# Projecting the queries of two token chunks as one Strassen pair, with three groups of loads held back until the keys have landed

## The chip, the cores and the metric

The kernel runs on one core of one Trainium2 chip. The metric is the device time of one execution in microseconds (us), lower being better. The span in a trace, from the first to the last instruction, is some 1.7 us shorter than that time.

## The reference

One transformer layer on 2048 tokens of width 1024, in bfloat16: layer norm, a projection to queries, keys and values, attention of 32 heads over 8 positions at a spacing of 2 (a token's own and seven earlier ones), an output projection with a residual, and a gated feed-forward part of inner width 3584 without an activation.

```python
qkv    = layernorm(x) @ wqkv                      # (2048 x 1024) @ (1024 x 3072)
idx    = pos[:, None] - 2 * arange(8)[None, :]    # 8 positions back from pos; negative ones masked
logits = einsum("bhsd,bhswd->bhsw", q, k[idx]) * 32 ** -0.5
o      = einsum("bhsw,bhswd->bhsd", softmax(logits), v[idx])
h      = x + o @ wo
# then, from layernorm(h): (g * u) @ w_down, with g = ln @ w_gate and u = ln @ w_up, added to h
```

## The kernel before

Tokens go in four chunks of 512. TensorE does all the matrix products. Attention itself runs on VectorE, a chunk at a time, out of a second layout: ScalarE evacuates q, k and v from PSUM, SyncE's queue stores them to device memory, and GpSimd's queue loads them back with heads and tokens spread over the 128 partitions. The result goes the same way: it is stored (`od`) and loaded transposed in quarters (`oT`), which the output projection reads. The order of everything is fixed when the kernel is built; work that isn't urgent sits in generators that are advanced as matmul groups are emitted. In the traces below each engine takes its instructions in that order (ScalarE's evacuations stood 8.30 us behind an issue, for instance), which the whole story turns on.

```python
# evacuation of one 128x512 group of q, k or v (ScalarE) and its store (SyncE)
def evac_qkv(c, m, ps):
    sg = t1k.tile([128, HB + TC], BF, ...)
    nc.scalar.copy(sg[:, HB:HB + TC], ps[:])
    ...
    nc.sync.dma_start(qd[c][...] or kd[c][...] or vd[c][...], ...)

# absolute sums over the down weights; the loads are issued by ScalarE itself
def abs_down():
    ring = wpool.tile([128, KO, 512], BF, tag="w", name="w_ring")
    def load(p):
        nc.scalar.dma_start(rows_of(p), wd_v[:, bass.ts(p, 4), 512:1024])
    for p in range(2):
        load(p)
    yield "later", 12.0
    for p in range(7):
        scale_d.add(p, rows_of(p), rows_of(p))          # ScalarE
        if p + 2 < 7:
            load(p + 2)
        yield "later", 4.9 * GROUP_US

# attention of one chunk, cut: products and sums to logits on VectorE, then
    nc.vector.tensor_tensor(lg[:], lg[:], mx..., ALU.subtract)
    nc.scalar.activation(lg[:], lg[:], ACTF.Exp, ...)   # the one step on ScalarE
    ...                                                 # sums, weights, products with v on VectorE
    nc.gpsimd.dma_start(od[c]..., oD[:])
    for cp in range(4):
        nc.gpsimd.dma_start(oT[:, :, cp, :], od[c][cp]...)

# the main order, cut
    qkv(0, range(1, 4))                 # block 0 came before; 0,1 are q, 2,3 k, 4,5 v
    load_qk(0)
    bg.finish(rows2)
    for t in range(4):
        norm1[2].transpose(t)           # SyncE
    xtiles[3] = load_x(3, "x", nc.sync)
    pump(6)                             # loads the value weights
    bg.add(norm1[3].sums(), bg.now + 18.0)              # chunk 3's layer norm, on ScalarE
    start_attention(0)
    sums = abs_down()
    bg.add(sums, bg.now + 25.0, first=True)
    qkv(1, range(4))
    qkv(0, range(4, 6))
    load_v(0)
    bg.add(norm1[3].rows(), bg.now, first=True)
    qkv(1, range(4, 6))
    ...
    qkv(2, range(6))
    qkv(3, range(4), last=True)         # each finished block frees a 1 MB slot for the next weights
    bg.finish(atts[0])
    nxt = wo_ln2(0)                     # first output projection and chunk 0's second norm
    qkv(3, range(4, 6), last=True)
```

## Time and profile before

| | before |
|---|---|
| time, median of 4 runs (span of those) | 770.38 us (770.09 to 770.49) |
| TensorE busy | 99% of the span |
| matmuls of q for chunks 2 and 3 | 128 of 512 columns |
| first output projection starts | 163.6 us |
| first quarter of its input lands | 147.97 us |
| second output projection starts | about 253.2 us |
| first quarter of its input lands | 248.09 us |

The prediction below shows the lines on what bounds this kernel. The timeline: start, length, engine and line, operation, output<-input, and in square brackets how long the engine had been idle and what released it. First ScalarE: the issue of two loads for the absolute sums, and the exponential of attention 0.

```profile
66.72 1.16 ACTq L671 DMA_DIRECT2D w_ring<-in_B_w_down_dram  x2
...
97.34 1.06 ACT L499 ACTIVATE lg<-lg 128x1024 f32<-128x1024 f32 x1
```

Then the first sum of the softmax on VectorE:

```profile
98.43 0.69 DVE L502 TENSOR_TENSOR trs<-lg 128x512 f32<-128x512 f32 x1 [1.12 <-ACT lg L499]
```

The issue of a load stands in ScalarE's own order like any other instruction. Here it cost ScalarE 1.6 us (the idle time of its next instruction, shown in the prediction), and VectorE waited 1.12 us for the exponential, hardly more than the 1.06 us that it lasts.

### The profile page before, as it was taken

What the parts mean: (1) busy time and instruction counts of PE and PEld (TensorE: products, weight loads), DVE (VectorE), ACT (ScalarE), POOL (GpSimd) and SP (SyncE); (2) the same over time, 40 slices, a digit from 0 to 9 for tenths busy, and PEclk for the clock granted to TensorE, in tenths of its full rate; (3) what the DMA queues carried; (4) which work ended last, traced back from release to release, by engine and by line L of the source; (5) the groups of instructions that cost most, each with busy time, mean ns of one, the idle gap of its engine ahead of it and who ended that gap; (6) DMA issues with size and microseconds to landing.
All of it is one profiled execution on the core that took longest, in us unless ns stands there. A gap on an engine that the chain in (4) does not pass through costs nothing.

```text
span 768.7 us, 10302 instructions
## 1 busy us (share of the span) xinstructions
PE 762.8 (99%) x3663; PEld 350.7 (46%) x3663; DVE 606.0 (79%) x718; ACT 513.1 (67%) x979; POOL 142.5 (19%) x152
## 2 busy tenths in 40 slices
PE   8999999999999999999999999999999999999998
PEld 5444444444444444444444444444444444444444
DVE  5639999999999999999998997975454444568863
ACT  4648966423687398778899986736777677788240
POOL 0000000200002000020000001018778677600000
PEclk9999999999999999999999999999999999999999
DMA  8999796999966699579559448674342423730001
GB/s 268 272 257 260 207 269 153 279 305 283 301 219 216 210 299 294 172 246 326 194 186 300 139 155 279 126 198 107 80 110 55 110 74 91 257 126 29 0 29 55
DMA packets 190915, 144.85 MB, mean 188 GB/s; under 512 B 81808, under 2 KB 181136, under 8 KB 188688
## 3 DMA queue, kind: packets, MB, share of 16 engines
q1 hardware_dynamic: 180416, 116.94, 54.2%
q0 software_dynamic: 3584, 22.02, 8.4%
q10 hardware_dynamic: 6864, 5.24, 2.5%
q8 instruction: 28, 0.46, 0.2%
q14 instruction: 23, 0.19, 0.1%
HBM read 110.10 MB, written 27.26 MB: 179 GB/s over the span
## 4 chain that ended last, share of the span: by engine, by line
PE 97%; DVE 2%; DMA 1%; issue 0%; ACTq 0%; DVEq 0%
PE ps L431 21%; PE dx L944 6%; PE pz L826 6%; PE pwu L431 6%; PE pu L431 6%; PE py L826 6%; PE pwg L431 6%; PE pg L431 6%; PE px L826 6%; PE wo L998 4%; PE pv L826 3%; PE ez L944 3%; PE ey L944 3%; PE ex L944 3%; PE dy L944 3%; PE wo L578 2%
## 5 line engine op out<-in xcount | busy, mean ns | idle before, releaser
L431 PE MATMUL ps<-lnT,w_qkv 128*128 128x512 bf16 x736 | 159.5, 379 | 0.0
L431 PEld LDWEIGHTS <-w_qkv 128*128 128x128 bf16 x736 | 71.9, 98 | 86.1 <-issue 0.2
L344 ACT CAST sg<-ps 128x512 bf16<-128x512 f32 x96 | 55.2, 586 | 46.9 <-PE ps L431 41.6
L477 DVE TENSOR_TENSOR prod<-qD,kD 128x4096 bf16<-128x4096 bf16 x32 | 72.2, 2284 | 12.8 <-DMA kD<-kd 12.8
L523 DVE TENSOR_TENSOR pv<-vD,at 128x4096 bf16<-128x4096 bf16 x32 | 72.4, 2285 | 0.2
L826 PEld LDWEIGHTS <-sw 128*128 128x128 f16 x448 | 43.8, 98 | 52.9 <-issue 0.2
L431 PEld LDWEIGHTS <-w_wu 128*128 128x128 bf16 x448 | 43.8, 98 | 52.9
L431 PEld LDWEIGHTS <-w_wg 128*128 128x128 bf16 x448 | 43.8, 98 | 52.9
L826 PE MATMUL px<-lnT,ws 128*128 128x512 bf16 x224 | 55.2, 379 | 0.0
L536 POOL DMA_DIRECT2D od<-oD x4 | 2.2, 544 | 275.6 <-DVE oD L534 275.6
L431 PE MATMUL pg<-lnT,w_wg 128*128 128x512 bf16 x224 | 52.9, 379 | 0.0
L431 PE MATMUL pu<-lnT,w_wu 128*128 128x512 bf16 x224 | 52.9, 379 | 0.0
L431 PE MATMUL pwu<-lnT,w_wu 128*128 128x512 bf16 x224 | 52.9, 379 | 0.0
L431 PE MATMUL pwg<-lnT,w_wg 128*128 128x512 bf16 x224 | 52.9, 379 | 0.0
L826 PEld LDWEIGHTS <-ws 128*128 128x128 f16 x336 | 32.9, 98 | 39.6
L807 POOL TENSOR_TENSOR sw<-ws 128x512 f16<-128x512 f16 x26 | 30.0, 1155 | 82.4 <-PE pv L826 49.1
L944 PEld LDWEIGHTS <-gs 128*128 128x128 f16 (+1 forms) x280 | 27.4, 98 | 33.0
L479 DVE TENSOR_TENSOR prod<-prod 128x4096 bf16<-128x4096 bf16 x16 | 36.6, 2288 | 0.4
L843 ACT COPY py<-px 128x512 f32<-128x512 f32 x28 | 16.0, 570 | 27.7 <-PE px L826 27.7
L808 POOL TENSOR_TENSOR sw<-sw,ws 128x512 f16<-128x512 f16 x26 | 30.0, 1154 | 2.0
L810 POOL TENSOR_TENSOR sw<-ws,sw 128x512 f16<-128x512 f16 x26 | 30.3, 1167 | 0.0
L809 POOL TENSOR_TENSOR sw<-ws 128x512 f16<-128x512 f16 x26 | 30.1, 1156 | 0.0
(334 smaller groups left out, 1472.9 us busy)
## 6 DMA issues: line engine op xcount, KB each, us to landing
w_wg<-in_B_w_gate_dram SPq DMA_DIRECT2D x14, 1024.0 KB, 6.9
w_wu<-in_B_w_up_dram SPq DMA_DIRECT2D x14, 1024.0 KB, 6.3
w_pair<-in_B_w_gate_dram SPq DMA_DIRECT2D x14, 512.0 KB, 4.0
w_pair<-in_B_w_up_dram SPq DMA_DIRECT2D x14, 512.0 KB, 5.3
w_wo<-in_A_wo_dram SPq DMA_DIRECT2D x6, 1024.0 KB, 7.6
w_qkv<-in_A_wqkv_dram SPq DMA_DIRECT2D x5, 1024.0 KB, 11.5
kd<-sg SPq DMA_DIRECT2D x32, 144.0 KB, 4.4
kD<-kd POOLq DMA_DIRECT2D x4, 1152.0 KB, 8.6
```

Of the source, the lines that this page charges most:

```text
L344: nc.scalar.copy(sg[:, HB:HB + TC], ps[:])
L431: nc.tensor.matmul(ps[:], lhsT=wt[:, ko, bass.ts(j, 128)], rhs=rhs[:, ko, :], start=(ko == 0), stop=(ko == KO - 1))
L477: nc.vector.tensor_tensor(prod[:, j], qD[:], kD[:, :, o:o + SUB], ALU.mult)
L479: nc.vector.tensor_tensor(prod[:, :, 0:16], prod[:, :, 0:16], prod[:, :, 16:32], ALU.add)
L523: nc.vector.tensor_tensor(pv[:, j], vD[:, :, o:o + SUB], at[:, w, None, :].to_broadcast((128, DH, SUB)), ALU.mult)
L807: eng.tensor_tensor(sw[:, i, 0], a21, a22, ALU.add)
L808: eng.tensor_tensor(sw[:, i, 1], sw[:, i, 0], a11, ALU.subtract)
L809: eng.tensor_tensor(sw[:, i, 2], a11, a21, ALU.subtract)
L810: eng.tensor_tensor(sw[:, i, 3], a12, sw[:, i, 1], ALU.subtract)
L826: nc.tensor.matmul(ps[:], lhsT=lhs[:, ko, :], rhs=rhs[:, ko, :], start=(fresh and ko == 0), stop=(ko == 3), skip_group_check=not fresh)
L944: nc.tensor.matmul(ps[:, bass.ds(lo, n)], lhsT=lhs[k][:, bass.ts(q, 128)], rhs=rhs[k][:, bass.ds(lo, n)], start=(fresh and k == 0), stop=( ...
L998: nc.tensor.matmul(ps[:], lhsT=oTs[c][:, kk, t, :], rhs=wts["wo", 2, hf][:, kk, :], start=(kk == 0), stop=(kk == KO - 1))
```

## The change

The intent is to save matmuls. Queries of chunks 2 and 3 are two products with the same weights, so they form a 2 x 2 block product, and Strassen's scheme needs 7 block products for 8. That takes sums of weights and of rows on VectorE, q weights scaled to float16 (so an absolute sum over them), and copies between PSUM banks. The pair needs the rows of both chunks and is placed behind the first output projection, which by the count of matmuls thereby comes 13.8 us earlier. The queries of chunk 2 come with it, so attention 2 is started behind it too. To get attention 0 started in spite of the added work, three groups of transfers that used to run beside the first k load now wait until it has landed. The core of the diff, cut at the dots:

```diff
-    qkv(0, range(1, 4))
-    load_qk(0)
+    qkv(0, [1], at={(1, k): (lambda k=k: q_abs(k)) for k in range(4)})   # 4 absolute sums, ScalarE
+    qkv(0, [2], at={(2, 2): scale_q.rows})
+    qkv(0, [3], at={(3, 2): scale_q.total, (3, 3): q_convert})
+    load_qk(0, after=lnTs[1][:, 0, TC - 1:TC])     # q load waits for chunk 1's transposes
+    start_attention(0)
+    qkv(1, [2])
     bg.finish(rows2)
+    w4 = wpool.tile([128, KO, 512], BF, tag="w", name="w_qkv_4")
+    nc.gpsimd.tensor_copy(w4[:, 0, 0:1], qkv_in["k", 0][:, 0, 0:1])      # the hold-back
+    pump(6, w4)
+    state["live"] += 1
+    xtiles[3] = load_x(3, "x", nc.sync)
     for t in range(4):
         norm1[2].transpose(t)
-    xtiles[3] = load_x(3, "x", nc.sync)
-    pump(6)
-    state["live"] += 1
-    bg.add(norm1[3].sums(), bg.now + 18.0)
-    start_attention(0)
+    bg.add(norm1[3].both(), bg.now + 20.0, first=True)   # sums and rows in one piece
     sums = abs_down()
-    bg.add(sums, bg.now + 25.0, first=True)
-    qkv(1, range(4))
+    bg.add(sums, bg.now + 18.0, first=True)
+    qkv(1, [3, 0, 1])
     qkv(0, range(4, 6))
     load_v(0)
-    bg.add(norm1[3].rows(), bg.now, first=True)
     qkv(1, range(4, 6))
 ...
-    qkv(2, range(6))
+    qkv(2, range(2, 6))
-    qkv(3, range(4), last=True)
+    qkv(3, range(2, 6), last=True)
     bg.finish(atts[0])
-    nxt = wo_ln2(0)
-    qkv(3, range(4, 6), last=True)
+    rows_q = q_row_sums()                          # 13 sums on VectorE
+    norm2 = [wo_norm(0, devs=False)]               # second norm of chunk 0, now on ScalarE
+ ...
+    for m0 in (0, 2):
+        q_pair(m0, room_q)                         # 2 x 2 Strassen blocks
```

## The prediction

> **What bounds the kernel now.** I read the page's busy shares first, then the chain that ended last, then everything the TensorE waited for, then single stretches of time.
>
> ```profile
> PE 762.8 (99%) x3663; PEld 350.7 (46%) x3663; DVE 606.0 (79%) x718; ACT 513.1 (67%) x979; POOL 142.5 (19%) x152
> ...
> PE 97%; DVE 2%; DMA 1%; issue 0%; ACTq 0%; DVEq 0%
> ```
> The TensorE is busy for 762.8 of 768.7 us, and 97% of the chain is its own work. That matmuls are merely in flight is not proof, so I looked at their spacing. In the chain in order of time (start, length, what):
>
> ```profile
> 27.20 136.41 PE ps L431 x632
> 163.61 13.81 PE wo L602 x64
> 177.42 13.81 PE ps L431 x64
> ```
> 136.41 us by 632 is 215.8 ns for each 128x512 matmul; 13.81 by 64 is the same. No pause separates the pieces, so from 27 to 191 us the array never waits. All its waits:
>
> ```profile
> PE warm_ps L338 <- DVE warm L324: 1.2, 1, 1.2
> PE pt L386 <- DVE ln L379: 0.8, 1, 0.8
> PE ps L392 <- DMA w_qkv<-in_A_wqkv_dram: 0.5, 1, 0.5
> PE ps L392 <- ACT lnT L387: 0.3, 1, 0.3
> ```
> All four fall in the first 16 us. So time is matmuls times spacing: a matmul removed gains 216 ns, and whatever makes the array wait costs its full length. There is nothing else to gain; the 12.8 us that VectorE idles at 39.6 to 52.3 cost nothing today.
>
> **What the skill says.** TensorE: Matmul & The Clock Gate, Back-to-back issue gap, gives N/2.4 + 2.5 ns for an isolated warm matmul, 215.8 for N=512; the trace agrees to the digit (its sustained 131 ns does not occur here). PSUM — Partial Sum Buffer, PSUM: the matmul accumulator, gives eight banks of 512 float32 columns; the kernel uses eight such tiles, so a product that can't get an evacuated bank waits. VectorE: DVE Perf Modes, The perf-mode tier table, gives a bf16 tensor_tensor of 2048 elements 1224 ns; the trace has 1222 (L481), so the Strassen sums are priced from it and from the 512-element float16 sums at 412 ns (L1112). DMA: Bandwidth & Descriptors, Issuing engines are not separate DMA queues, says that all transfers interleave on the same 16 engines. The trace agrees: chunk 1's first transpose landed 3.35 us after issue, the next, issued 0.4 us after the 1 MB q load, took 7.66.
>
> **The change: TensorE.** Before, q for chunks 2 and 3 is 2 chunks x 8 column tiles x 8 = 128 matmuls. After, it is 4 Strassen blocks x 7 products x 4 = 112. 16 fewer by 0.2158 = 3.45 us gained. One 64-column matmul for the weights' scale is added; at the 56 ns that 128 columns take in this trace, about 0.03. Net 3.42 us, that is 767.0 us if nothing waits.
>
> **ScalarE at the start.** Four absolute sums over the q weights are added, priced from this group, with the read of the accumulator 1.90 each, 7.6 in all:
>
> ```profile
> L635 ACT ACTIVATE w_ring<-w_ring 128x2048 bf16<-128x2048 bf16 x7 | 13.4, 1912 | 0.0
> ```
> They stand between the evacuations of 17 to 30 us, where ScalarE idled 3.6 us. It comes to issuing chunk 1's two late transposes at about 33.5 instead of 29.75 us. The recorded bank waits are all met: the tightest is the bank freed by the q evacuation at about 27.7, wanted at 30.5. The array wants chunk 1's transposes at 39.1. The old ones landed at 38.88, with 0.2 us to spare; the new second one goes at 34.9, and since the q load now waits for it, should take 3.4 and land at 38.3. No stall, 0.8 us of margin.
>
> **Start of attention.** The last k store goes 3 us later (43.1 for 40.04), its load issues at about 46.2 for 44.12. Freed of the 2 MB of value weights, 1 MB of rows and the transposes that come behind it now, it should take 6.8 for 8.12 and land at 53.0, where it landed at 52.24. VectorE has by then converted the q weights (2 x 1.25) and made 16 weight sums (6.1), ending at about 50.6, inside its old idle time. So the hold-back only pays for the delays.
>
> **The output projection is 13.8 us earlier.** 16 q groups (27.6) move behind it and 8 value groups (13.8) before it: it starts at 149.6, not 163.6. Attention 0 took 84.2 us of VectorE from the first product to the last sum (52.34 to 136.55), then 11.4 until the first transposed quarter landed (147.97). From 53.0: 148.6. Margin 1.0, where it was 15.6. The value weights should land near 63 for 66.7.
>
> **ScalarE in the Strassen pairs.** This is where I expect to lose. A bank is copied to the next by ScalarE inside each pair:
>
> ```profile
> L843 ACT COPY py<-px 128x512 f32<-128x512 f32 x28 | 16.0, 570 | 27.7 <-PE px L826 27.7
> L848 ACT ACTIVATE p<-pv,ibgu 128x512 f32<-128x512 f32 x28 | 19.2, 687 | 7.6 <-PE pv L826 7.6
> ```
> Two blocks take 56 matmuls, 12.1 us. On ScalarE they need 6 copies and 6 scaled evacuations, 12 x about 0.55 occupied = 6.6. In the same first 12 us the layer norm of chunk 0 now runs there instead of on VectorE: these pieces (chunk 3's norm, same shapes)
>
> ```profile
> 67.93 1.06 ACT L274 ACTIVATE njunk<-x 128x1024 bf16<-128x1024 bf16 x1 [1.60 <-DMA kd<-sg]
> 71.91 1.15 ACT L279 ACTIVATE njunk<-x,nroom 128x1024 bf16<-128x1024 bf16 x1
> 85.41 1.24 ACT L296 ACTIVATE ln<-x,nroom,rs 128x1024 bf16<-128x1024 bf16 x1
> ```
> give about 2.5 us a row tile for sum, mean and square, 1.3 for the four scales, 1.14 a row written. Three of the four row tiles are meant to be done in the projection. But each waits for VectorE's residual add, and VectorE runs late here:
>
> ```profile
> 167.89 4.49 DVE L477 TENSOR_TENSOR prod<-qD,kD 128x4096 bf16<-128x4096 bf16 x2
> 172.30 1.28 DVE L604 TENSOR_TENSOR h<-wo,h 128x512 bf16<-128x512 f32 x2
> ```
> The first add came 7.0 us after its group was done at 165.3. In the changed order it comes after 104.0 us of attention work, at 53.0 + 104.0 = 157.0, 5.7 late. The first row tile is then ready at 158.3, and three tiles end at 165.9. The first copy between banks is behind them, ends at 166.5, and is wanted at 166.0: 0.5 lost. The fourth tile (2.5) stands between two copies: the second block's third bank is ready at 171.8 for 170.9, 0.9 lost. The scales, then two written rows, cost about 0.1 each time. I laid the two queues end to end by hand: 1.7 us lost, pairs from 163.4 to 189.3 where 24.2 would do. VectorE's own row sums (12 x 0.4 + 1.2) end at 167.7, wanted at 168.3, so they just pass.
>
> **Sum.** 770.4 - 3.45 + 0.03 + 1.7 = 768.7; the rounded call is 768.6.
>
> **Rivals.** *Everything hides*: the order was made with care, and most margins above are positive by calculation; then 767.0. Against it: ScalarE has 6.6 + 2.5 + 1.3 + 2 x 1.14 = 12.7 us for 12.1 in the first pair, before any lateness. *ScalarE loses the whole gain*: if k lands 1 us later, at 54, every add is a microsecond later and the pairs lose about 3 us; with a microsecond from the transposes, 771. For it speak the 0.8 and 1.0 us margins, each worked out from one landing. *VectorE becomes the bound*: 15 us of conversions and sums plus 6 of evacuations are added, 8.4 of norm removed; the 12.8 us of idle take them up. It would enter the gated stage about 3.6 us later than before. The second projection has slack: its first quarter landed at 248.09 for 253.2. Minus the lateness and the 1.7 net shift, near zero remains; a miss would cost 0 to 2. *The hold-back itself gains*: k earlier frees VectorE, but VectorE idles off the chain, so no time.
>
> **Range and chances.** Floor 767.0 by the count of matmuls; executions differ by 0.14 us. The losses I add are 0 to 4 us, most likely 1 to 2.5. So 766.8 to 771.4 for 8 in 10. Two per cent is 15.4 us: the gain can't reach it, and a loss would need stalls of 19 us, a wait I missed altogether.
>
> **What would show it.** TensorE with 3648 matmuls. Its list of waits, empty after 16 us before, should show only the new bank tiles of the pairs (the y and z banks) released by ScalarE, 1 to 3 us in sum, and the pairs some 26 us long. The k load should land at 52 to 54 us. Chunk 1's matmuls and the first projection should start without a wait. It is wrong if the pairs take 24.2 us (copies in time), if the waits lie at the start (scale matmul, chunk 1's transposes, value weights) or at either projection, or if the sum of TensorE's waits is above 5 us.

## The result, and the profile after

The changed kernel takes 783.09 us (median of 4, 781.95 to 784.36); the kernel before took 770.38 in the same rounds. The ratio is 1.0166, with a 95% interval of 1.0148 to 1.0184. Ratios here are the mean time of one kernel's fast runs over that of the other's of the same rounds, so not quite the ratio of the medians. The class, within 2%, was as predicted; the sign was not, and 783.09 lies far outside 766.8 to 771.4.

The page of the changed kernel, busy shares and then the shares of the chain that ended last:

```profile
PE 763.7 (98%) x3648; PEld 349.7 (45%) x3648; DVE 620.9 (79%) x748; ACT 538.4 (69%) x1017; POOL 142.7 (18%) x154
...
PE 37%; DVE 35%; ACT 11%; DMA 6%; issue 5%; SPq 2%; ACTq 0%; DVEq 0%; POOL 0%; POOLq 0%
```

The count of 3648 matmuls is as predicted. But the chain now runs through TensorE for 37% only, where it was 97%. TensorE's busy time even rose by 0.9 us although it does 15 matmuls fewer: the page counts a matmul that runs slowly as busy too, which is 2.3 us here (below). The rest of the rise is not accounted for. TensorE's waits (engine, line and tile, what released it: total, times, longest):

```profile
PE wo L646 <- DMA oT<-od: 7.2, 1, 7.2
PE ps L480 <- ACT halo L399: 2.8, 2, 2.1
...
PE ez L1069 <- DVE hsr L787: 1.1, 1, 1.1
PE qz L934 <- ACT qz L974: 0.8, 1, 0.8
```

I also took the excess of each interval between starts of matmuls over 0.4217 ns a column. The large pieces are 2.25 us at 99.5 and 0.83 at 112.5 (a bank not evacuated by ScalarE), 7.36 at 153.1 (the first output projection, waiting for `oT`), 2.29 right behind it, 1.0 in the pair and 1.27 at 510. With a further 1.1 us of small pieces that is 16.1 us lost; 3.4 saved makes 12.7. The spans differ by 781.5 - 768.7 = 12.8.

The 2.29 us is a matter of clock: the granted clock was 0.86 of full speed from 160.6 to 177.0 us, where it was 1.00 in this stretch before. The projection's line in TensorE's timeline:

```profile
160.63 16.29 PE L646 MATMUL wo<-w_wo,oT 128*128 128x512 bf16 x64 [7.19 <-DMA oT<-od]
```

The same 64 matmuls took 13.81 us before. After the pause, ten of them started 426 or 427 ns apart instead of 216, and one 400.

Where `oT` came from, in the chain in order of time (start, length, what):

```profile
145.98 6.63 DMA od<-oD
...
153.17 7.41 DMA oT<-od
```

Attention 0 ended at 145.7 us, not at the predicted 137.2, and the trip through memory took 14.6 us from issue of the store to the first quarter. In the kernel before, GpSimd's timeline has the same issues closer together:

```profile
136.85 0.54 POOL L536 DMA_DIRECT2D od<-oD  x1 [47.11 <-DVE oD L534]
141.35 3.55 POOL L539 DMA_DIRECT2D oT<-od  x4 [3.96 <-DMA od<-oD]
```

There the store had landed at 141.06, and the first quarter at 147.97.

Attention 0 began about as predicted: the k load landed at 54.09 (predicted 53.0). The time went in the middle. VectorE:

```profile
97.90 1.23 DVE L551 TENSOR_TENSOR lg<-lg,mx 128x1024 f32<-128x1024 f32 x1
107.56 0.69 DVE L556 TENSOR_TENSOR trs<-lg 128x512 f32<-128x512 f32 x1 [8.44 <-ACT lg L553]
```

Its logits were ready at 99.1, and it then sat 8.44 us until the exponential was done. ScalarE, which owed it:

```profile
68.44 5.90 ACTq L674 DMA_DIRECT2D w_ring<-in_B_w_down_dram  x2
74.39 0.69 ACT L392 ACTIVATE sg<-ps,ibq 128x512 bf16<-128x512 f32 x1 [8.30 <-PE ps L480]
74.97 1.05 ACT L277 ACTIVATE njunk<-x 128x1024 bf16<-128x1024 bf16 x1
...
106.47 1.06 ACT L553 ACTIVATE lg<-lg 128x1024 f32<-128x1024 f32 x1
```

Read the second of these with care. ScalarE was idle for 8.30 us, and the line names TensorE as the releaser; but its group had been done for long. What stood there is the line above: the issue of the two w_ring loads, which the chain of waits shows released by a store of chunk 1's k. That store had stood in SyncE's queue, behind loads and transposes:

```profile
58.10 9.71 SPq L234 DMA_TRANSPOSE lnT<-ln  x4
67.92 2.65 SPq L406 DMA_DIRECT2D kd<-sg  x4
```

From 74.97 to the exponential ScalarE has no pause to speak of. It works through evacuations, absolute sums and the whole norm of chunk 3, four sums, four squares and four rows, all ahead of the exponential in its order. That order is not new: in the kernel before, too, the four rows (85.4 to 94.9) came ahead of the exponential (97.3). But there the sums had begun at 59.1, three of them ahead of the w_ring issue; now all stand behind it and begin 15.9 us later.

### The profile page after: what moved, and what is told of

Same layout as the page of the kernel before. It is cut to its first block, busy times and chain, and to the rows that moved or that the text cites.

```text
span 781.5 us, 10340 instructions
## 1 busy us (share of the span) xinstructions
PE 763.7 (98%) x3648; PEld 349.7 (45%) x3648; DVE 620.9 (79%) x748; ACT 538.4 (69%) x1017; POOL 142.7 (18%) x154
## 4 chain that ended last, share of the span: by engine, by line
PE 37%; DVE 35%; ACT 11%; DMA 6%; issue 5%; SPq 2%; ACTq 0%; DVEq 0%; POOL 0%; POOLq 0%
DVE pv L577 8%; PE dx L1069 6%; PE px L829 6%; PE pz L829 6%; PE py L829 6%; DVE prod L531 4%; DVE pv L586 3%; PE pv L829 3%; DVE oD L588 3%; PE dy L1069 3%; PE wo L646 2%; DVE prod L533 2%; DMA b21r<-in_B_w_down_dram 2%; PE ez L1069 2%; ACT sg L394 1%
## 5 line engine op out<-in xcount | busy, mean ns | idle before, releaser
L480 PE MATMUL ps<-lnT,w_qkv 128*128 128x512 bf16 x608 | 132.4, 379 | 2.8 <-ACT halo L399 2.8
L480 PEld LDWEIGHTS <-w_qkv 128*128 128x128 bf16 (+1 forms) x608 | 59.3, 98 | 74.4 <-issue 3.9
L394 ACT CAST sg<-ps 128x512 bf16<-128x512 f32 x72 | 41.7, 584 | 18.1 <-PE ps L480 14.1
L810 POOL TENSOR_TENSOR sw<-ws 128x512 f16<-128x512 f16 x26 | 30.0, 1153 | 79.9 <-PE py L829 72.9
L646 PE MATMUL wo<-w_wo,oT 128*128 128x512 bf16 x128 | 30.3, 401 | 7.2 <-DMA oT<-od 7.2
```

What stands on the lines that cost most here:

```text
L480: nc.tensor.matmul(ps[:], lhsT=wt[:, ko, bass.ts(j, 128)], rhs=rhs[:, ko, :], start=(ko == 0), stop=(ko == KO - 1))
L646: nc.tensor.matmul(ps[:], lhsT=oTs[c][:, kk, t, :], rhs=wts["wo", c, hf][:, kk, :], start=(kk == 0), stop=(kk == KO - 1))
L810: eng.tensor_tensor(sw[:, i, 0], a21, a22, ALU.add)
```

## The experiments

Names used in the expectations: theory H, the stand at the w_ring load makes the exponential late; rival R, the norm of chunk 3 in front of it does so whatever the load does; rival S, the Strassen part itself, with the margin at the projection, is too dear. Theories T, M and V came later. "Sum of waits" is the sum of matmul spacing as above.

### The two halves of the change, each alone

`strassen_alone` puts the old order of loads back into the changed kernel:

```diff
-    load_qk(0, after=lnTs[1][:, 0, TC - 1:TC])
-    start_attention(0)
-    qkv(1, [2])
-    ... gate on w4, pump(6, w4), load_x(3), transposes, norm1[3].both() ...
-    qkv(1, [3, 0, 1])
+    load_qk(0)
+    ... transposes, load_x(3), pump(6), norm1[3].sums(), as before ...
+    qkv(1, [2, 3, 0, 1])
     qkv(0, range(4, 6))
     load_v(0)
+    bg.add(norm1[3].rows(), bg.now, first=True)
```

> Undoes the hold-back: the Strassen pair stays, with its absolute sums, its scaling and the early projection; chunk 2's transposes, chunk 3's rows and the value weights are issued in the old order, without a wait. Theory H (the hold-back makes the SyncE queue late, so that ScalarE stands 8.3 us in front of the w_ring load; chunk 3's norm and then the Exp of attention 0 come late, and the projection waits): ScalarE has no stand above 3 us between 60 and 80 us, the Exp comes within 2 us of its logits, the first projection waits under 2 us. But the k load has the old traffic beside it, 8.1 us from its issue at 48, so it lands near 56; the time is 768 to 772, best guess 770. Rival S (the Strassen part itself costs: the projection is 13.8 us earlier than attention 0 allows, and ScalarE is too full in the pairs): the projection still waits 5 us or more, and the time is 778 or above.

Measured: 781.28 us (778.21 to 783.28), ratio 1.0132 (1.0102 to 1.0163). A miss for theory H in its form, and the place was wrong for both theories. TensorE's waits:

```profile
PE ps L480 <- ACT halo L399: 4.4, 1, 4.4
PE ps L480 <- DMA lnT<-ln: 2.3, 1, 2.3
```

There is no wait at the first projection. By then the array was late already: it had waited 2.3 us at 39.0 for chunk 1's transposes, which without the gate on the q load travel beside it again, and 4.4 us at 112.3 for a bank. That bank hung on ScalarE, which stood twice at w_ring loads, 6.81 us ahead of 75.3 and again here:

```profile
116.15 0.59 ACT L394 CAST sg<-ps 128x512 bf16<-128x512 f32 x1 [7.23 <-DMA w_ring<-in_B_w_down_dram]
```

What stood was the issue, at last done at 115.68, of the next load; it waited for an earlier one of its own ring, in flight for 16 us (99.61 to 115.61), mostly beside the 1 MB loads of q, k and v. Behind the 4.4 us pause eleven matmuls again ran at 426 or 427 ns. So the hold-back is not the cause of the stand at w_ring; it also happens without it, with other releasers.

`hold_alone` is the reverse: the kernel before, and in it only the gate, the order of loads and the placement of chunk 3's norm.

```diff
-    load_qk(0)
-    ... old order ...
+    load_qk(0, after=lnTs[1][:, 0, TC - 1:TC])
+    ... gate on w4, new order, norm1[3].both(), as in the changed kernel ...
```

> The kernel before with the hold-back alone: 128 q matmuls in the old place, no absolute sums, projection at 163.6 us. Theory H: ScalarE again stands about 8 us before the w_ring load, the Exp is again several us late (VectorE idle before the softmax sums 5 to 9 us), but the old margin of 15.6 us at the projection takes that up; only the bank waits of 99 and 113 us remain, about 3 us, so 771 to 774.5, best guess 773. Rival S: nothing of it matters, 770.4 within 0.7. If it is 778 or more, the hold-back costs all by itself and the lost margin has no part in it.

Measured: 774.06 us (773.0 to 775.24), ratio 1.0043 (1.0028 to 1.0058). The time is as theory H had it, two details are not. The stand was 3.6 us, not 8, and the array lost its time elsewhere. VectorE's softmax sums:

```profile
102.59 0.69 DVE L508 TENSOR_TENSOR trs<-lg 128x512 f32<-128x512 f32 x1 [6.62 <-ACT lg L505]
```

The exponential was late by nearly as much as in the changed kernel, though the stand was less than half as long. Its norm of chunk 3 began at 69.9, where it had begun at 59.1. That speaks for rival R as a second contributor. The old margin of 15.6 us at the projection took the lateness up, as expected; 2.0 us came out behind it, where the gate matmuls wait for chunk 0's second norm. So, by the medians of the same rounds, the hold-back alone costs 3.5 us and Strassen alone 10.7; together they cost 12.7, a little less than the sum. The larger part of the loss comes with the Strassen half, even under the old order of loads.

### What makes the exponential late

`ring_pool`: the changed kernel, w_ring loads from GpSimd's queue.

```diff
-            nc.scalar.dma_start(rows_of(p), wd_v[:, bass.ts(p, 4), 512:1024])
+            nc.gpsimd.dma_start(rows_of(p), wd_v[:, bass.ts(p, 4), 512:1024])
```

> The changed kernel with one edit: the loads of the w_ring tile are issued from GpSimd's queue and not from ScalarE's, so that ScalarE can't stand behind them. Theory H: the first sum of chunk 3's norm starts by 68 us (74.97 in the changed kernel), VectorE idles under 2 us before the softmax sums (8.44), the projection waits under 2 us (7.2), no matmuls at half speed behind it, bank waits at 99 and 113 us under 0.5; the time is 768 to 771, best guess 769.3. Rival R (chunk 3's norm, placed in one piece ahead of the Exp, fills ScalarE whatever the load does): the Exp still comes 4 us or more after its logits, 774 to 780. Rival S: 778 or above.

`rows_later`: the changed kernel, the four rows of chunk 3's norm moved behind the exponential.

```diff
         def both(self):
             yield from self.sums()
+            yield "later", 14.0
             yield from self.rows()
```

> The changed kernel with the four row writes of chunk 3's norm 14 us later in ScalarE's order, behind the Exp; the w_ring load still blocks ScalarE. Theory H: the stand of 8.3 us stays, the backlog at the Exp is shorter by the 4 x 1.24 us of rows, so VectorE idles 3 to 4 us before the softmax sums, the projection waits 1.5 to 4 us, the time is 773 to 779, best guess 776. Rival R: the placement of the rows was the cause, the Exp is on time (idle under 1.5 us), 769 to 771.

Measured: `ring_pool` 776.97 us (776.31 to 779.38), ratio 1.0086 (1.0064 to 1.0108); `rows_later` 775.79 us (775.12 to 777.45), ratio 1.0068 (1.0052 to 1.0083). The softmax sums on VectorE in `ring_pool`:

```profile
100.35 0.69 DVE L556 TENSOR_TENSOR trs<-lg 128x512 f32<-128x512 f32 x1 [1.86 <-ACT lg L553]
```

In `rows_later` the same step starts at 104.20, after 4.24 us of idle.

Both edits help, and by about the same: 6.1 and 7.3 us. In `ring_pool` the wait of 8.44 fell to 1.86 and the bank waits at 99 and 113 us are gone, so the stand is shown to be a cause. In `rows_later` the stand was even longer (9.56 us), and the wait still fell by 4.2 us; that the backlog of the norm in front of the exponential was too long once the stand had delayed it is shown to be the other. Neither theory is the whole. In `ring_pool` the first sum of the norm still began at 68.84, 9.7 us later than in the kernel before, and the exponential was only 0.8 us late: without the stand the later placement is nearly harmless, since ScalarE then gets through its queue in time. A part of the gain of `rows_later` is clock: its profiled execution was granted 1.000 and has no matmuls at half speed behind the projection's pause of 1.9 us, while `ring_pool` has eight after its 6.3 us.

The time of `rows_later` was as expected, that of `ring_pool` a miss (768 to 771 expected), and it held a surprise. Attention 0 ended at 138.5 us, and the projection still waited 6.3. The chain of `ring_pool`:

```profile
138.76 9.23 DMA od<-oD
...
148.28 7.46 DMA oT<-od
```

That is 17.0 us for a trip that took 11.1 in the kernel before (store issued at 136.85, first quarter landed at 147.97), and 12.7 in `rows_later`.

### Where the trip's time goes

Each finished block of chunk 3 frees a slot, and the next 1 MB of weights is loaded at once. With the value blocks moved ahead of the projection these loads fall into the trip: in `ring_pool` two of the output weights, issued at 130.0 and 137.7, then gate and up weights at 144.1 and 148.2. `ring_pool_held` adds this to `ring_pool`, `held_only` adds it to the changed kernel:

```diff
-    pump(pair_at)
+    pump(8)                              # no further than the output weights
     ...
     bg.finish(atts[0])
+    state["limit"] = pair_at
+    while state["live"] < 7:
+        wt = wpool.tile([128, KO, 512], BF, tag="w", ...)
+        nc.gpsimd.tensor_copy(wt[:, 0, 0:1], oTs[0][:, 0, 3, 0:1])   # wait for the last quarter
+        pump(state["next"] + 1, wt)
```

> As ring_pool, and the loads of the first gate and up weights (1 MB each) wait until the last quarter of attention 0's transposed result has landed. In ring_pool attention 0 ended on time (138.5 us), yet its result took 17.0 us from issue of the store to the first quarter (138.76 to 155.74), 11.4 by the prediction. Theory T (those early weight loads share the 16 DMA engines with the trip): the store, which has only the output weights beside it, takes 7 to 9 us, the first quarter 6.5 us, it lands at 152.5 to 154.5, the projection waits 3 to 5 us (6.3 before), time 772.5 to 775.5, best guess 774. If the weight loads are not what stretches the trip, the wait stays above 6 us and the time at 776 to 778.

> The changed kernel with the gate and up loads held until oT has landed, the w_ring load left on ScalarE. Theory H plus T: the Exp stays 7 us late and attention 0 still ends near 145.7; the trip to the first quarter shrinks from 14.6 to 11.5 to 13 us, the projection waits 4.5 to 6 us (7.2), bank waits at 99 and 113 us unchanged; time 779 to 782, best guess 781. If the trip isn't stretched by those loads, 783 as it was.

Measured: `ring_pool_held` 773.42 us (772.69 to 774.86), ratio 1.0041 (1.0026 to 1.0056); `held_only` 779.12 us (778.47 to 780.15), ratio 1.0114 (1.0099 to 1.0129). The chain of `ring_pool_held`:

```profile
139.05 8.51 DMA od<-oD
...
147.84 4.27 DMA oT<-od
```

Theory T holds. Without the feed-forward weights beside it the first quarter takes 4.27 us for 7.46, and both kernels gain 3.6 to 4 us; in `held_only`, whose exponential stays late, the trip shrank from 14.6 to 10.9 us and the wait from 7.2 to 3.4. The store's 8.5 us stays: an output weight of 1 MB, which the projection itself needs, is in flight from 137.7 to 144.2. The kernel before stored its `od` in 4.2 us at this very time, with rows of x beside it in place of weights. And in `sums_on_pool` below, where the store is issued at 154.90, after the output weights and the stores of v have landed, it takes 4.17 us again and the first quarter 4.02. So what travels beside the store stretches it; whether that is the weights or the stores of v is not separated.

### Margin, or the cost of the pair?

`pair_first` is `ring_pool` with half of the pair ahead of the projection (cut; a count of free slots moves too, so one weight load comes later):

```diff
+    bg.finish(rows_q)
+    q_pair(0, room_q)
     norm2 = [wo_norm(0, devs=False)]
-    bg.finish(rows_q)
 ...
-    for m0 in (0, 2):
-        q_pair(m0, room_q)
+    q_pair(2, room_q)
```

> As ring_pool, but the first half of the Strassen pair (56 matmuls, 12.1 us) runs ahead of the output projection instead of behind it, so that the projection has that much margin again; one weight load (w_wu) comes later too. Theory M (what is lost at the projection is lost margin, not the Strassen work): no wait for oT, no matmuls at half speed, the copies between banks in time in the first half since no layer norm stands among them; but the norm of chunk 0 has only one half of a pair to hide behind, so the first gate matmuls wait 2 to 6 us for their transposes. Time 769 to 774, best guess 771.5. Rival S (the Strassen pair itself costs): 776 or above, with the waits inside the pairs.

Measured: 796.48 us (795.2 to 797.4), ratio 1.0338 (1.0321 to 1.0355), the worst of all. My 771.5 was wrong. Its waits:

```profile
PE pg L480 <- DMA lnT<-ln: 13.7, 1, 13.7
PE qv L934 <- DVE qt L917: 8.7, 4, 7.9
```

There is indeed no wait for `oT` any more, and in the first half, with no norm among its copies, ScalarE's copies hardly hold the array up. But VectorE, deep in attention 1, made the row sums 8 us too late, and the norm of chunk 0, with 12 us of pair to hide behind instead of 24, came 13.7 us late. The experiment was too coarse to price the margin; it shows that either order of these two pieces waits on VectorE or on a norm behind it.

Two smaller steps from `ring_pool_held`. `held_swap` lets ScalarE make the copy that TensorE waits for first:

```diff
             p5[i] = room[:, m0 + i, :]
-            nc.scalar.activation(p5[i], v[:], ACTF.Copy, scale=inv)
             q_product(yb[i], sw[i][1], t2, False)
             zb[i] = bank("z", i)
             nc.scalar.copy(zb[i][:], yb[i][:])
+            nc.scalar.activation(p5[i], v[:], ACTF.Copy, scale=inv)
```

> As ring_pool_held; in each pair ScalarE copies the y bank to the z bank before it scales the v bank, not after. The second z copy of the first pair is then 0.6 us earlier, so the 1.1 us that the array lost there in ring_pool_held should fall to 0.4 to 0.6, and the time from 773.4 to 772.5 to 773, unless the v bank, freed later, is missed by the u product. If the layer norm of the fourth row tile between the copies is not what delays them, nothing changes.

`x_first` adds to it that the first two products of the pair, which need no row sums, run ahead of the projection:

```diff
+    first = q_first(0)                  # x products of the first pair, with their copies to y
     norm2 = [wo_norm(0, devs=False)]
 ...
-    for m0 in (0, 2):
-        q_pair(m0, room_q)
+    q_pair(0, room_q, first)
+    q_pair(2, room_q)
```

> As held_swap, and the first two products of the first pair (8 matmuls, 1.73 us, they need nothing of VectorE's row sums) run ahead of the output projection, with their copies to the y banks. The projection is wanted 1.73 us later, so its wait of 2.75 us for oT should fall to 0.8 to 1.3 us, with no matmuls at half speed. Sum of the waits after 17 us about 2 us: time 769 to 771, best guess 769.8, so about level with the kernel before; if the margin were not what costs, the time stays at 772.7.

Measured: `held_swap` 774.32 us (772.74 to 776.27), ratio 1.005 (1.0033 to 1.0068), no gain over `ring_pool_held`, whose interval overlaps (772.5 to 773 expected). `x_first` 779.38 us (776.34 to 780.3), ratio 1.011 (1.0092 to 1.0128): a loss of 5 us where I expected to win some 3. By an estimate from the runs, about 1.4 us of it goes with the clock: the five executions of `x_first` took 776.3 and 777.0 us at a granted clock of 1.000 and 0.998, and 779.4 to 780.3 at 0.995 or 0.996, and `held_swap` took 772.7 and 773.2 at 1.000 and 0.998. At equal clock the loss is 3.6 to 3.8 us. The waits of `x_first` that matter:

```profile
PE wo L646 <- DMA oT<-od: 3.7, 2, 2.8
PE ey L1085 <- DVE gs L1253: 1.9, 1, 1.9
...
PE ez L1085 <- DVE hsr L787: 1.0, 1, 1.0
```

In `held_swap` the z copy is as late as ever (a wait of 0.8 us, as before), since a row tile's sum, mean and square stand in front of it, and the u bank became late in addition (0.5). In `x_first` the wait at the first projection did fall, from 2.76 us to 1.04 by the spacing, just as expected. What I had not counted is the rest: `oT` is now waited for twice, the second time at the second projection (2.95 us at 251.6), and two waits for VectorE follow at 464 and 504 us. Behind the first of them (2.1 us) seven matmuls ran at 426 or 427 ns. The array had come earlier to a place that VectorE was not earlier at.

### VectorE behind the waits

In `x_first` VectorE works from 139.05 to 241.36 us, from the end of attention 0 to the end of attention 1, and is idle for 2.3 us of these 102.3 (what no instruction of its covers). In the kernel before the same stretch lasted 100.6 us with 3.4 idle. The sums by stretch, first of the kernel before, then of `x_first` (length, then busy time of TensorE, its weight loads, VectorE, ScalarE and GpSimd):

```profile
136.80:237.40 100.60, 100.60 (x468) 45.59 (x466) 97.25 (x90) 51.69 (x114) 5.72 (x8) 1.00 0.94 274
```

```profile
139.00:241.40 102.40, 100.22 (x457) 45.42 (x465) 100.11 (x96) 71.75 (x136) 7.41 (x12) 1.00 0.86 256
```

So the theory V: once the first waits are mended, VectorE sets the end. `sums_on_pool` moves 12 of the 13 row sums to GpSimd:

```diff
-            nc.vector.tensor_tensor(t1[k], b12[:, k, :], b11[:, k, :], ALU.subtract)
-            nc.vector.tensor_tensor(t2[k], b22[:, k, :], t1[k], ALU.subtract)
+            nc.gpsimd.tensor_tensor(t1[k], b12[:, k, :], b11[:, k, :], ALU.subtract)
+            nc.gpsimd.tensor_tensor(t2[k], b22[:, k, :], t1[k], ALU.subtract)
 ... likewise t4; emitted before qkv(3, range(2, 6))
```

> As x_first, and 12 of the 13 row sums of the pair (5.0 us of VectorE) go to GpSimd, which does nothing between 119 and 139 us; at 1.15 us each, from the sums of the same shape there, they take about 14 us. Theory V (after the first waits are mended, VectorE is what sets the end: it has hardly an idle microsecond from 139 to 480 us, and what the array gains ahead of the second projection it gives back there, 2.95 us in x_first, and again at 464 and 500 us): the second projection waits under 0.5 us, the waits of 464 and 500 us shrink to under 1 us together, time 769 to 773, best guess 770.8. If VectorE isn't the bound, the second projection still waits 2 us or more and the time stays at 776 to 780. A third way: sums on GpSimd slow VectorE's own work beside them, attention 0 ends more than 0.5 us later than 139.05, and the wait moves to the first projection.

Measured: 783.31 us (782.35 to 783.85), ratio 1.0165 (1.0152 to 1.0179). The third way, and far worse than I had allowed for. GpSimd's and VectorE's timelines:

```profile
120.27 3.08 POOL L918 TENSOR_TENSOR qt<-lnT,qt 128x512 f16<-128x512 bf16 x1
```

```profile
116.89 2.29 DVE L586 TENSOR_TENSOR pv<-pv 128x4096 bf16<-128x4096 bf16 x1
...
128.69 3.13 DVE L586 TENSOR_TENSOR pv<-pv 128x4096 bf16<-128x4096 bf16 x1
```

A GpSimd sum of the shape that takes 1.15 us later in these traces took 3.1, a VectorE operation of 2.29 us took 3.13, and both ended late: VectorE's attention 0 at about 147.6, GpSimd's sums at 154.9. As the store of `od` stands behind those sums in GpSimd's order, it was issued 16 us late, and the first projection waited 12.1 us. The Trainium skill, SBUF — State Buffer, section Who interferes with whom, gives a reason: the two engines share one pair of ports, held as an exclusive lock, and a VectorE instruction with two inputs in SBUF contends with GpSimd reading. The trace agrees that they contend, with the numbers above. For theory V this run decides little, since the array was 12 us late when it came to the second projection.

`no_sums` asks the same question without that side effect. It leaves the row sums out, so its result is wrong:

```diff
-        t1, t2, t4 = ... 12 subtractions on VectorE ...
-        nc.vector.tensor_tensor(t3, b22, b12, ALU.subtract)
+        t1, t2, t4 = ([b[:, k, :] for k in range(4)] for b in (b11, b22, b21))
+        t3 = b12
```

> As x_first, with the 13 row sums of the pair left out (the products read unsummed rows): the result is wrong on purpose, the TensorE work and every transfer are the same, VectorE has 6.2 us less to do before the second projection and GpSimd nothing more. Theory V: the second projection waits under 0.3 us (2.95 in x_first), the waits of 464 and 500 us under 0.6 together (3.2), the first projection 1.0 as before; time 768 to 771, best guess 769.5, so even without that work hardly better than the kernel before. If VectorE isn't the bound, 776 to 780 as x_first.

Measured: 769.44 us (769.26 to 769.91), ratio 0.9987 (0.997 to 1.0004). Its waits:

```profile
PE wo L646 <- DMA oT<-od: 1.0, 1, 1.0
PE qz L925 <- ACT qz L973: 0.9, 1, 0.9
```

The second projection no longer waits, and the waits at 464 and 504 us are gone. Attention 1 ended 5.8 us earlier (235.55 for 241.36), and its first quarter landed at 247.6 for 254.7. What differs from `x_first` is 6.2 us of VectorE work (and the wrong values), and by the medians it was worth 10 us; between the two profiled executions, with clocks of 0.998 and 0.999, it is 7.5. Theory V is shown. It also sets a limit: even with the sums free of charge and most waits mended, the pair is only 1.3 us ahead of the kernel before, with an interval (0.997 to 1.0004) that includes no gain. I found no version with a right result that beats the kernel before; the best was `ring_pool_held`, 0.4% behind it.

## Why the prediction was wrong, step by step

**TensorE, right.** 3648 matmuls and 3.4 us saved. With the waits taken off, the span of the changed kernel comes to 781.5 - 16.1 = 765.4, which is 768.7 - 3.4 to 0.1 us.

**ScalarE at the start, right.** (The four absolute sums are a little dear of their price: the 1.91 us of the line is without the read of the accumulator, with it a sum took 2.0.) Chunk 1's transposes were issued at 33.36 and 34.83 and landed at 36.82 and 37.98, ahead of 39.1; no stall. `strassen_alone` shows what the gate on the q load is for: without it 2.3 us are lost there.

**Start of attention, nearly right.** The k load was issued at 48.10 for 46.2, took 6.0 us for 6.8 and landed at 54.09 for 53.0. The value weights landed at 59.5 and 62.5, in time.

**"Attention 0 took 84.2 us of VectorE from the first product to the last sum": the step that failed.** I carried a duration over from the old order to the new as if it were VectorE's own. It contains one hand-over to another engine, the exponential, and that engine's queue had been changed. It took 91.5 us (54.22 to 145.68), 7.3 more, for the 8.44 us of idle where 1.12 had been. I had laid out what ScalarE does up to 47 us and in the pairs; from the stretch of 60 to 107 us I had taken prices only. I had asked neither what the load issue in it waits for nor what stands in front of the exponential when chunk 3's norm begins behind that issue, 15.9 us later than before.

**"Then 11.4 until the first transposed quarter landed": failed too.** It was 14.9, and 17.2 in `ring_pool`, counted like the 11.4 from the end of VectorE's last sum. That number also belonged to its surroundings: the projection and the weight loads that follow it moved 13.8 us ahead, into the trip. The skill's remark on shared DMA engines was quoted in the prediction and used for the k load and the first transposes only.

**"Margin 1.0": so there was none.** (By its own terms it is 1.2: 163.6 - 13.8 is 149.8, not 149.6.) The array wanted `oT` at 153.2 (itself 3.5 late from the bank waits), and had it at 160.6. A fair reading of two numbers that each hung on other queues would have put several us of doubt on that margin, and the upper end of the range far above 771.4.

**ScalarE in the pairs, about right.** 1.3 us lost for 1.7, and the wait is named as foretold, the z bank released by ScalarE. The agreement is in part luck: the working had VectorE's first residual add 5.7 us late, and since the projection itself slipped by 11 us the add came only some 1.4 us late. The loss was real but among the smallest of those listed below. Expecting it to be the main one was the wrong emphasis.

**The sum.** To 767.0 I added 1.7, for the pair alone. The trace has 7.4 at `oT`, 2.3 of slow matmuls behind it, 3.5 around the two bank waits, 1.3 in the pair, 1.3 at 510 and 0.4 elsewhere, 16.2 in all by these rounded pieces. Both of the signs that the prediction named for itself came: a wait at the first projection, and a sum far above 5 us.

**The rivals.** "VectorE becomes the bound" was given 0 to 2 us. In the changed kernel it didn't come to that, since the array was later still. But `x_first` and `no_sums` show that it is what stands behind: mend the rest, and it takes the gain. "The hold-back itself gains: no time" was right in that it doesn't gain; alone it costs 3.5 us. "ScalarE loses the whole gain" hung on k landing at 54, and k did land at 54.09; but the pairs lost no more than 1.3, with the projection later still.

**What stays open.** Why the store of chunk 1's k that released the w_ring load came so late is read from SyncE's timeline, not tested by itself; nor is it shown why the issue of a weight load should wait for a store of k at all, since releasers are inferred from semaphore events. The runs of `x_first` spread from 776.3 to 780.3 with their granted clock (1.000 down to 0.995), but why some executions lose clock at their pauses and others don't is not known; only one of them is in a trace. Of the trip's remaining 8.5 us for the store it is shown that it is the company, not which part of it. And `strassen_alone`, the larger half of the loss, was not taken apart by runs of its own.

## What to carry to other kernels

A duration between two events on one engine can be carried to a new order only after every hand-over inside it has been looked at: list what the other engine has in front of the piece that is waited for, the issue of loads included. A load issued by a compute engine is an instruction of that engine, and the engine stands as long as that issue has to wait (8.30 us here). And before a saving on the busiest engine is counted, find how far the second busiest can follow: here 3.4 us of saved matmuls needed 6.2 us of sums on a VectorE that with them had 2.3 us of idle time in 102.

## What the Trainium skill lacked or had wrong

- SBUF — State Buffer, Who interferes with whom: of VectorE's two-port modes it says that the loser of the shared ports blocks fully, of an instruction with two inputs in SBUF only that it contends. Over a run of the latter neither side won: in `sums_on_pool` a GpSimd sum went from 1.15 to 3.1 us and a VectorE operation from 2.29 to 3.13. The page has no figure for what such a steady overlap costs both.
- TensorE: Matmul & The Clock Gate, section Part 1: The HAM clock gate (the "warmup" mystery): it gives 426.7 ns for a matmul of 512 columns at the low clock, which the traces have to the digit (426 to 427 ns, ten matmuls after the 7.2 us pause). It ties the low clock to an idle window of about 3.4 us. Here a pause of 2.75 us in `ring_pool_held` was also followed by six matmuls at 426 or 427 ns, and one of 2.76 us at the same place in `held_swap` by none. In `x_first` a pause of 2.1 us was followed, 1.3 us on, by seven. So a shorter pause is no safety. After pauses of 2.1 to 13.9 us the slow matmuls cost 1.2 to 2.7 us on top of the pause, where there were any.
- DMA: Bandwidth & Descriptors, Issuing engines are not separate DMA queues: it says that the time a sequencer spends on issuing a transfer is usually small beside the transfer. It leaves out that an issue may have to wait while the engine stands: 8.30 us of ScalarE in the changed kernel, for two half-megabyte loads. Moving all loads of this tile to GpSimd's queue was worth 6.1 us.
- The same page has no figure for how an ordinary transfer stretches beside ordinary loads and stores: the 1 MB store of `od` took 4.2 us in the kernel before and 9.2 in `ring_pool`.
